# ScalarE makes the first part of p for the third block of rows

## The chip, the cores and the metric

The kernel runs on one core of a Trainium2 chip. The metric is the device time of one execution in microseconds (us). A core has a matrix engine (TensorE, PE in the profile; its weight loads are PEld), VectorE (DVE), ScalarE (ACT), GpSimd (POOL) and SyncE (SP), whose queue issues the DMAs here. Each engine takes its instructions in order; between engines they wait for semaphores.

## The reference

Three layers in a row. Attention with a decay for 4 batches of 8 heads, sequence 576, head width 64:

```python
scores = scale * np.matmul(q, k.transpose(0, 1, 3, 2))
decay = cum[:, :, :, None] - cum[:, :, None, :]      # cum: running sum of log f
scores = np.where(causal, -1000000000.0, scores + decay)
attn = np.exp(scores - max); attn = attn / (sum + 1e-09)
out = np.matmul(attn, v)
```

Then a first MLP (512 to 2048 and back, with a leaky ReLU that has a slope per column), and a second one (512 to twice 1536, the two halves multiplied, back to 512), over 2304 tokens.

## The kernel before

The work is float32 throughout; most products are made of two or three products of rounded parts. 32 heads pass through attention one after the other, numbered n, in steps u = 0 to 33. The 576 rows of a head are four blocks of 128 rows (i = 0 to 3) and a rest of 64, which two heads share (i = 4). Causality makes block i 128 x (i + 1) wide, so the third block (i = 2) is 128x384.

One step works on three heads: it makes the scores of head u and their exponentials (ops s0 to s3; VectorE takes the scores from PSUM, adds the mask and finds the maximum, L385; ScalarE takes the exponential and its sum, L386), normalises head u - 1 and turns it (ops h0 to h4 and l0 to l4), and multiplies head u - 2 by v (p0, p1). Op T turns q and k of head u + 1 (L338) and copies them out of PSUM in parts (L346 to L358). Op ri, first in each step, makes the reciprocals of the sums on VectorE (L408, L409); the h ops need them.

The normalised exponentials are called p. There are two kinds of heads:

- In the first ten heads (n below NATIVE, 10) p stays whole. Op h multiplies s by the reciprocal in place (L421 to L428), op l transposes it on TensorE (L449) and copies it out of PSUM.
- In the other 22 heads p is split into two half precision parts. Op h makes the first part, s times the reciprocal rounded to 16 bits (L436 to L440); op l makes the second, the remainder, on VectorE (L520). When both blocks of a group are done, a DMA transposes the group (L527). Blocks 2 and 3 are one group, p_hi, blocks 0 and 1 another, p_lo.

Which engine runs an op is read from a table by `eng`. Its default for the h ops is GpSimd:

```python
def eng(key, default):
    d = _P["eng"]
    if ap_["u"] < _P.get("es", 0):
        d = dict(d, **_P.get("eng0", {}))
    return {"pool": pool, "act": act, "dve": dve}[d.get(key, default)]
```

`es` is 10: in steps 0 to 9 the entries of `eng0` are laid over the table. `eng0` has no entry for h2.

The strings `even`, `odd`, `even0` and `odd0` list the ops of a step in the order in which the text issues them; h2 stands behind h3 in the odd steps and in the later even ones. Op M, once step 10 is reached, lets blocks of the first MLP in between, at a rate that the table fixes, so that TensorE has work while softmax runs; op W rounds weights. The MLP blocks use ScalarE for a ReLU and a rounding copy (L668, L670), VectorE for the leaky sum (L669) and GpSimd for the remainder (L671). The text's order gives priorities; the framework's scheduler, which keeps a timeline of its own costs (L1078), writes the order of each engine's queue from them, and adds the semaphores.

After attention the rest of the first MLP and then the second run, which the table does not touch.

Of the kernel before, what the change touches and what calls it, by code (L numbers as in the profile page):

```python
# [40 lines left out]
    odd="ri h3 h2 h0 R rr vs h1 M Q l2 T l3 s2 M h4 s3 l1 M M s1 l0 s0 p0 p1 V W po l4 M".split(),  # L41
    split=0,
    lag=2,
    eng={'U': 'pool', 'xl': 'pool', 'h0': 'pool', 'h1': 'pool', 'nq': 'act', 'x': 'dve'},
    psm=3,
    first=10,
    rates=[0, 1, 1, 1, 0.8, 1.15, 1.15, 0.95],
# [1034 lines left out]
```

## Time and profile before

| | us |
|---|---|
| median of 3 runs | 1085.79 (1085.08 to 1087.99) |
| profiled execution | 1083.83 |
| its span, first to last instruction | 1082.0 |
| TensorE busy | 1027.9 |
| VectorE busy | 719.0 |
| ScalarE busy | 473.8 |
| GpSimd busy | 516.8 |

Busy time is the union of an engine's instructions; the rest of the span is idle time, and the profile names for it what the next instruction waited for. The granted clock is the share of TensorE's full speed that it was given: it has two levels, 2.4 and 1.2 GHz, and its mean over the execution was 0.992.

### The profile page before, as it was taken

The page shows a single profiled execution, that of the slowest core. Times are in us where ns is not written, and L with a number is a line of the kernel's source. Part 1 is how long each engine was busy: PE and PEld are TensorE (multiplying, and loading weights), DVE is VectorE, ACT ScalarE, POOL GpSimd, SP SyncE. Part 2 cuts the span into 40 slices and gives each one's busy share as a digit, 9 for nine tenths or more (in the row PEclk, how much of TensorE's full clock was granted, in tenths as well). Part 3 has the DMA queues.
Part 4 walks back from the last instruction along what each step waited for, and adds up shares of the span by engine and source line. Part 5 has one row for each costly group of instructions (what it writes and reads, how often), then busy time and mean ns, then how long its engine had stood idle before and what let it go on. Part 6 is the DMA issues. An engine that isn't in the chain of part 4 may idle for free.

```text
span 1082.0 us, 18604 instructions
## 1 busy us (share of the span) xinstructions
PE 1027.9 (95%) x6447; PEld 963.6 (89%) x6447; DVE 719.0 (66%) x1518; ACT 473.8 (44%) x1168; POOL 516.8 (48%) x598
## 2 busy tenths in 40 slices
PE   5989999999999999999999997899999999999998
PEld 3868888898888899999999996899989999899997
DVE  6667988888888456444456358654986568974553
ACT  5777767767675454333344443322433113321110
POOL 4444767667676356333446667522443223541111
PEclk9999899999999999999999999999999999999999
DMA  5546575875775676666666997636327483354623
GB/s 113 154 101 193 123 132 123 201 146 116 176 163 100 165 262 192 192 223 199 191 215 227 355 365 257 238 134 253 108 88 254 155 301 126 124 183 172 241 86 111
DMA packets 221697, 196.26 MB, mean 181 GB/s; under 512 B 138980, under 2 KB 195812, under 8 KB 221604
## 3 DMA queue, kind: packets, MB, share of 16 engines
q1 hardware_dynamic: 221604, 195.08, 60.0%
q8 instruction: 51, 0.84, 0.3%
q14 instruction: 42, 0.34, 0.1%
HBM read 126.83 MB, written 50.17 MB: 164 GB/s over the span
## 4 chain that ended last, share of the span: by engine, by line
PE 55%; DVE 5%; POOL 2%; DMA 2%; issue 2%; ACT 1%; SPq 0%; ACTq 0%; DVEq 0%; POOLq 0%
PE p L674 7%; PE p L676 7%; PE p L675 7%; PE o L676 4%; PE o L675 4%; PE o L674 4%; PE hb L674 4%; PE ya L675 3%; PE hb L676 3%; PE hb L675 3%; PE ya L676 3%; PE ya L674 3%; DMA wr_in<-in_moe_w_in 1%; POOL yhl L881 1%; POOL g L671 0%
## 5 line engine op out<-in xcount | busy, mean ns | idle before, releaser
L674 PE MATMUL p<-yq,w_h 128*128 128x384 f32 x360 | 122.4, 340 | 4.7 <-DVE td L1031 2.3
L675 PE MATMUL p<-yq,w_h 128*128 128x384 f32 x360 | 121.8, 338 | 0.0
L676 PE MATMUL p<-yq,w_h 128*128 128x384 f32 x360 | 121.2, 338 | 0.0
L1015 POOL TENSOR_TENSOR gg<-tc,gg 128x384 fp32r<-128x384 f32 x36 | 36.6, 1017 | 113.2 <-ACT gg L1014 102.9
L674 PE MATMUL o<-w_o,gg 128*128 128x512 f32 x216 | 85.2, 396 | 3.4 <-ACT gg L1014 3.4
L675 PE MATMUL o<-w_o,gg 128*128 128x512 f32 x216 | 85.6, 396 | 0.0
L671 POOL TENSOR_TENSOR gb<-lt,gb 128x384 fp32r<-128x384 f32 x54 | 56.0, 1038 | 60.3 <-ACT gb L670 60.2
L676 PE MATMUL o<-w_o,gg 128*128 128x512 f32 x216 | 84.0, 394 | 0.5 <-POOL gg L1015 0.5
L386 ACT ACTIVATE s<-s,nm 128x512 f32<-128x512 f32 (+3 forms) x128 | 71.5, 559 | 26.3 <-DVE nm L385 25.2
L1015 POOL TENSOR_TENSOR gg<-td,gg 128x384 fp32r<-128x384 f32 x36 | 37.6, 1044 | 93.2 <-ACT gg L1014 87.4
L674 PEld LDWEIGHTS p<-yq,w_h 128*128 128x128 f32 x360 | 68.0, 189 | 9.4 <-issue 2.2
L669 DVE SCALAR_TENSOR_TENSOR lt<-lu,nal,hb 128x384 f32<-128x384 f32 x54 | 33.0, 612 | 61.5 <-ACT lu L668 61.5
L1014 ACT CAST gg<-tc 128x384 fp32r<-128x384 f32 x36 | 18.5, 514 | 123.8 <-DVE tc L1013 123.3
L675 PE MATMUL ya<-gb,w_out 128*128 128x384 f32 x216 | 72.7, 337 | 0.0
L676 PE MATMUL ya<-gb,w_out 128*128 128x384 f32 x216 | 72.3, 336 | 0.0
L674 PE MATMUL h<-xh,w_in 128*128 128x288 f32 x224 | 68.0, 307 | 3.5 <-DVE lt L669 3.5
L674 PE MATMUL ya<-gb,w_out 128*128 128x384 f32 x216 | 71.2, 335 | 0.0
L675 PEld LDWEIGHTS p<-yq,w_h 128*128 128x128 f32 x360 | 67.8, 188 | 3.5
L675 PE MATMUL y<-g,w_out 128*128 128x288 f32 x224 | 67.7, 306 | 2.0 <-POOL g L671 1.8
L674 PE MATMUL y<-g,w_out 128*128 128x288 f32 x224 | 66.8, 307 | 1.4 <-DVE lt L669 1.0
L676 PEld LDWEIGHTS p<-yq,w_h 128*128 128x128 f32 x360 | 67.5, 188 | 0.2
L675 PE MATMUL h<-xl,w_in 128*128 128x288 f32 x224 | 66.9, 300 | 0.1
(206 smaller groups left out, 3318.3 us busy)
## 6 DMA issues: line engine op xcount, KB each, us to landing
yq<-yq_d SPq DMA_DIRECT2D x49, 768.0 KB
yq_d<-yhl SPq DMA_DIRECT2D x42, 384.0 KB
yl<-ya_d SPq DMA_DIRECT2D x48, 192.0 KB
po_d<-os SPq DMA_DIRECT2D x36, 256.0 KB
os<-po_d SPq DMA_DIRECT2D x36, 256.0 KB
wr_in<-in_moe_w_in SPq DMA_DIRECT2D x16, 512.0 KB
wr_out<-in_moe_w_out SPq DMA_DIRECT2D x16, 512.0 KB
wr_a<-in_moe_w_a SPq DMA_DIRECT2D x12, 512.0 KB
```

The costliest lines, as they stand in the source:

```text
L386: act.activation(s, s, AF.Exp, bias=nm, scale=-1.0, accum_out=sm)
L669: dve.scalar_tensor_tensor(t, u, nal[:, fi:fi + 1], hp[:, :n], op0=ALU.mult, op1=ALU.add)
L671: pool.tensor_tensor(gl, t, f32(gh), op=ALU.subtract)
L674: pe.matmul(o, lh, rh, start=start, stop=False)
L675: pe.matmul(o, lh, rl, start=False, stop=False)
L676: pe.matmul(o, ll, rh, start=False, stop=stop)
L881: pool.tensor_tensor(yh[:, 1], x, f32(yh[:, 0]), op=ALU.subtract)
L1014: ap_["last"] = act.copy(g[:, 0], o).ins
L1015: pool.tensor_tensor(g[:, 1], o, f32(g[:, 0]), op=ALU.subtract)
```

## The change

One entry is added to the table, so that `eng("h2", "pool")` returns ScalarE:

```diff
-    eng={'U': 'pool', 'xl': 'pool', 'h0': 'pool', 'h1': 'pool', 'nq': 'act', 'x': 'dve'},
+    eng={'U': 'pool', 'xl': 'pool', 'h2': 'act', 'h0': 'pool', 'h1': 'pool', 'nq': 'act', 'x': 'dve'},
```

`p_hi` (L417) reads it in both of its branches. In either, GpSimd's product of s with the reciprocal becomes ScalarE's activation Copy with the reciprocal as its scale:

```python
if e is act:
    act.activation(t[:, 0::2, :], s, AF.Copy, scale=ri)
else:
    e.tensor_scalar(t[:, 0::2, :], s, ri, 1.0, op0=ALU.mult, op1=ALU.mult)
```

## Rows read from the trace of the kernel before

**Rows 1.** The page: busy time, share of the span and instructions.
```profile
PE 1027.9 (95%) x6447; PEld 963.6 (89%) x6447; DVE 719.0 (66%) x1518; ACT 473.8 (44%) x1168; POOL 516.8 (48%) x598
```

**Rows 2.** Windows: stretch, length, busy us of each engine, clock, DMA share, GB/s.
```profile
24.00:118.00 94.00, 87.28 (x553) 72.23 (x552) 65.47 (x206) 69.76 (x194) 46.61 (x65) 1.00 0.52 143
118.00:362.00 244.00, 226.14 (x1966) 213.04 (x1964) 210.54 (x559) 166.34 (x491) 166.34 (x238) 0.99 0.68 142
124.00:136.00 12.00, 10.79 (x56) 10.23 (x56) 11.32 (x35) 9.85 (x31) 7.34 (x10) 0.72 0.76 166
364.00:368.00 4.00, 4.00 (x21) 4.00 (x20) 0.00 (x0) 0.80 (x2) 0.00 (x0) 0.57 0.47 104
```

**Rows 3.** TensorE's waits: 118 to 362 us, then two of 24 to 118.
```profile
PE pv L542 <- DVE nm L385: 5.3, 9, 1.7
PE h L674 <- DVE lt L669: 2.9, 2, 1.5
PE sc L372 <- DVE nm L385: 2.6, 4, 1.0
PE pv L542 <- ACT TU L234: 2.0, 4, 0.7
...
PE sc L369 <- ACT PT_hi L234: 1.0, 2, 0.8
PE tp L449 <- POOL w_out L140: 0.8, 1, 0.8
```

**Rows 4.** Groups of GpSimd by form: busy us, mean ns, idle before.
```profile
L440 POOL TENSOR_SCALAR p_hi<-s,ri 128x384 f16<-128x384 f32 x22 | 12.9, 584 | 0.0
L427 POOL TENSOR_SCALAR s<-s,ri 128x384 f32<-128x384 f32 x10 | 6.2, 615 | 4.6 <-DVE ri L409 4.6
```

**Rows 5.** Timeline, end of attention: start us, us, instruction, idle before it.
```profile
359.03 0.58 POOL L440 TENSOR_SCALAR p_hi<-s,ri 128x384 f16<-128x384 f32 x1
362.84 0.78 POOL L671 TENSOR_TENSOR g<-lt,g 128x288 fp32r<-128x288 f32 x1
363.67 0.40 PE L675 MATMUL y<-g,w_out 128*128 128x288 f32 x1 [1.82 <-POOL g L671]
```

**Rows 6.** Line 427 on GpSimd: who waited for it (us, times).
```profile
  PEld tp L449: 2.2, 2
```

**Rows 7.** Groups of ScalarE by form, 118 to 362 us.
```profile
L386 ACT ACTIVATE s<-s,nm 128x384 f32<-128x384 f32 x21 | 12.9, 615 | 11.0 <-DVE nm L385 10.4 <-POOL p_lo L440 0.6
L234 ACT CAST xh<-x 128x320 fp32r<-128x320 f32 x10 | 4.6, 461 | 0.8 <-DVE x L576 0.5
```

**Rows 8.** Timeline of ScalarE and VectorE around the head at 288 us.
```profile
284.73 0.62 ACT L386 ACTIVATE s<-s,nm 128x384 f32<-128x384 f32 x1
285.25 0.19 ACT L386 ACTIVATION_READ_ACCUMULATOR s<-s,nm 128x1 f32 x1
287.61 0.38 ACT L575 ACTIVATE x<-pv 64x256 f32<-64x256 f32 x1
287.82 0.18 DVE L409 RECIPROCAL ri<-sm 128x4 f32<-128x4 f32 x1
288.49 0.41 ACT L234 CAST xh<-x 128x256 fp32r<-128x256 f32 x1 [0.51 <-DVE x L576]
```

**Rows 9.** Windows: the two microseconds behind ri in two heads.
```profile
152.50:154.50 2.00, 2.00 (x17) 2.00 (x16) 0.94 (x3) 1.90 (x7) 1.87 (x3) 1.00 1.17 203
322.50:324.50 2.00, 1.40 (x13) 1.19 (x11) 1.11 (x2) 1.90 (x5) 1.43 (x3) 1.00 0.73 176
```

**Rows 10.** Timeline of GpSimd and VectorE in two heads.
```profile
145.02 0.75 DVE L520 SCALAR_TENSOR_TENSOR p_hi<-s,ri,p_hi 128x512 f16<-128x512 f32 x1
...
288.83 0.59 POOL L440 TENSOR_SCALAR p_hi<-s,ri 128x384 f16<-128x384 f32 x1
288.89 1.06 DVE L520 SCALAR_TENSOR_TENSOR p_hi<-s,ri,p_hi 128x512 f16<-128x512 f32 x1 [0.43 <-POOL p_hi L440]
```

**Rows 11.** Groups of VectorE by form, 118 to 362 us.
```profile
L520 DVE SCALAR_TENSOR_TENSOR p_hi<-s,ri,p_hi 128x512 f16<-128x512 f32 x22 | 21.6, 981 | 5.4 <-POOL p_hi L440 5.3
```

**Rows 12.** Line 440 on GpSimd: duration ns min/median/max.
```profile
L440 POOL TENSOR_SCALAR p_lo<-s,ri x44: 365/772/1052, 119.8 to 360.4; 128x128 f16<-128x128 f32 x22, 128x256 f16<-128x256 f32 x22
```

## The prediction

> **What bounds the kernel now.** I read the page's busy line first, then the windows by stage, then who TensorE waits for. The busy line [rows 1] shows TensorE busy in 95% of a 1082.0 us span, VectorE in 66%, ScalarE in 44%, GpSimd in 48%; the average hides the stages. The change acts only while attention runs, up to about 362 us. There [rows 2] TensorE is busy 87.3 of 94 us between 24 and 118 us (the heads with whole p, no MLP blocks yet to fill in) and 226.1 of 244 us between 118 and 362 us (the heads with split p, interleaved with MLP blocks). So 6.7 and 17.9 us of TensorE idle are what can be won there at most, beside a slower clock; the matmuls themselves are fixed by the text. In the second stretch VectorE is busy 210.5 of 244 us, ScalarE and GpSimd 166.3 each. The waits of TensorE [rows 3] say which neighbour is late: the three largest entries are VectorE's (5.3 + 2.9 + 2.6 = 10.8 of the 17.9 us), the largest of ScalarE's is 2.0. In the first stretch ScalarE's entry is 1.0 and GpSimd's 0.8, both single or double stalls. VectorE is the neighbour that sets the pace of the split heads, ScalarE and GpSimd have some 78 us of slack each.
>
> **The change, part by part.** The key h2 is read at one place for both kinds of head, and the early table of engines does not overrule it. So all 32 heads move, the ten with whole p as well as the 22 with split p, though the words speak of the split ones alone. Nothing else is added: no DMA, no tile, no buffer.
>
> *What GpSimd loses.* 22 x 0.584 = 12.9 us in the split heads and 10 x 0.615 = 6.2 us before them [rows 4]. GpSimd is not the bound, so this counts only where something waits for it. One place is plain: at the end of attention GpSimd makes h2 of the last head at 359.03, four more instructions after it, and at 362.84 the subtraction that TensorE has been waiting for since 361.85; TensorE resumes at 363.67 after 1.82 us idle [rows 5]. Without h2 this comes 0.58 us sooner: -0.6 us (bounds 0, if ScalarE's part delays it instead, and -1.82). The other is at the start: TensorE's weight loads for the transposes waited twice, 2.2 us together, for GpSimd's rows of p [rows 6], and GpSimd makes the rows of one head one after the other. Two stalls shorter by up to 0.58 us each is -1.2 at best; I take -1.0 (bounds 0 and -1.2).
>
> *What ScalarE gains.* No row shows a scaled copy of 128x384 from SBUF to half precision. From above it is bounded by the exponential of the same 128x384, 0.615 us, which also takes a per-partition operand; from below by the 128x320 rounding copy, 0.461 us, with fewer columns and no such operand [rows 7]. The nearest is the exponential. Its neighbours overlap it: started at 284.73, its successor began at 285.25 [rows 8], so 0.52 us of the queue is what I charge: 22 x 0.52 = 11.4 us and 10 x 0.52 = 5.2 us. It waits for the reciprocal ri on VectorE. What is queued behind it on ScalarE: the copies of the next head's q and k out of PSUM, the high part of x, the ReLUs and rounding copies of the MLP, later the exponentials. VectorE and then TensorE wait for these. In the head at 288 us there is a hole for it: ScalarE ends its copy of x at 287.99 and idles 0.51 us until 288.49 while ri is ready at 288.00 [rows 8]. In the heads whose ri comes at 152.5 and at 322.5 there is none: ScalarE is busy 1.90 of the next 2.00 us [rows 9]. Going through all 22 in this way, 8 have no hole over 0.15 us within 2 us of ri, and these two are the first and last of them. So 8 x 0.52 = 4.2 us is pushed on; I let a quarter reach TensorE, taking that half of what stands behind it (the exponentials) is waiting for VectorE in any case, and that half of what is then late finds TensorE still with work: +1.05 us (bounds 0 and all 11.4). In the ten early heads ScalarE is busier, 69.8 of 94 us [rows 2], and a quarter of 5.2 is +1.3 (bounds 0 and 5.2).
>
> *What VectorE gains.* Behind h3 on GpSimd comes h2, and in the same moment VectorE starts the low part of the fourth block, which reads the same SBUF. At 288.83 GpSimd starts h2 (0.59 us) and at 288.89 VectorE starts l3, which takes 1.06 us; the l3 at 145.02, with no h2 beside it, takes 0.75 [rows 10]. The mean over 22 is 0.981 [rows 11]. So at most 22 x (0.981 - 0.75) = 5.1 us of VectorE's time goes. But GpSimd then does the next product, h0, at that moment, and l3 meets this one: I let half return, and half of the rest reach TensorE, since VectorE also idles (33.5 of 244 us, [rows 2]): -1.25 us (bounds 0 and -5.1).
>
> The Trainium skill (SBUF — State Buffer, "Who interferes with whom") says that a VectorE instruction with two SBUF inputs and a GpSimd instruction that reads SBUF exclude each other, the first to start keeping the shared port for its whole length, and that ScalarE has ports of its own. The 1.06 against 0.75 us agrees in direction, though the surplus, 0.31, is less than the 0.53 us that h2 still had to run. By this rule h0 (0.37 us at its shortest [rows 12]) would block l3 in h2's place, so an estimate from the rule keeps 0.59 - 0.37 = 0.22 us per head, 4.8 us on VectorE, and by the same halving -2.4 instead of -1.25: the sum would be -1.65.
>
> *The sum.* -0.6 - 1.0 + 1.05 + 1.3 - 1.25 = -0.5 us. The profiled execution took 1083.83 us (span 1082.0 and 1.8 around it), so it would be 1083.3; the median shown is 1085.79, 1.96 above the profiled one, so I predict 1085.3 for the median. The order that the framework's scheduler writes is worked out anew with the moved instruction, so these terms will not fall exactly where they do now; the ends below are wide for that.
>
> **The rivals.** *Faster: VectorE's relief goes through whole.* Nearly all of TensorE's stalls in the split heads are released by VectorE [rows 3]; if each head's stall shrinks by what VectorE saves, -5.1 stands for -1.25. The stall at 363.67 [rows 5] is followed by four microseconds at a mean granted clock of 0.57, so mostly at the lower of the two levels, 1.2 GHz [rows 2]: 4 x 0.43 = 1.7 us lost; a shorter stall may spare it. Sum: -5.1 - 0.6 - 1.7 - 1.0 + 1.05 + 1.3 = -6.05, 1079.7. For it: rows 3. Against: ScalarE's waits for VectorE are long, so the chain has slack in it.
>
> *Slower: ScalarE's queue becomes the late one.* ScalarE takes its instructions in order, and h2 can't start before ri. Where it is put ahead of the q and k copies, they stand behind its wait and its 0.52 us, the next head's scores start late, and TensorE has no scores to fill with. If half of it reaches TensorE in all heads, 32 x 0.52 / 2 = +8.3 stands for the +2.35: 8.3 - 0.6 - 1.0 - 1.25 = +5.45, 1091.2. It decides from the point where more than about half of the heads have no hole on ScalarE (8 of 22 now). One more stretch like 124 to 136 us, 12 us at a mean clock of 0.72 [rows 2] after TensorE had stalled, would add 12 x 0.28 = 3.4. For it: ScalarE's 74% in the early heads. Against: 14 heads with a hole, and ScalarE's slack of 78 us.
>
> *It does not do what it says:* if the ten early heads stay on GpSimd, +1.3 - 1.0 falls away: -0.8, 1085.0. The code speaks against it.
>
> **How the numbers follow.** 0.3% is 3.3 us, about what can be told from no change here; it separates 1082.5 and 1089.1. Chances: the forecast 0.37, the faster rival 0.35, the slower 0.23, the last 0.05 (it falls within 0.3%). So faster 0.35, the same 0.42, slower 0.23. The ends of the unknown terms reach from -9.8 (-1.82 - 1.7 - 1.2 - 5.1) to +16.6 (11.4 + 5.2), but all on one side at once is unlikely; 1078 to 1092 takes in both rivals' values with about 1 in 10 left on either side. The forecast's own range is 1082.5 to 1089.
>
> **What would show it.** Right: 32 activations of 128x384 on ScalarE of 0.55 to 0.62 us, none on GpSimd; GpSimd's busy time between 118 and 362 us down by some 13 us, ScalarE's up by as much; l3's mean between 0.75 and 0.95 us; the idle of TensorE in both stretches within 3 us of 6.7 and 17.9; the stall before the last subtraction 0.6 us shorter; nothing moved after 404 us but its start. Wrong: TensorE's waits for ScalarE (TU, T, N, PT) above 6 us in the split heads, as the slower rival wants; or TensorE's waits for VectorE under 7 us, as the faster one does; or a stretch at the lower clock that comes or goes, which moves the time by 2 to 3 us whatever these terms do.

## The result, and the profile after

The changed kernel takes 1072.12 us (median, 1068.47 to 1075.31) against 1086.89 for the kernel before, timed beside it: a ratio of 0.9874, 95% interval 0.9846 to 0.9902. That is 13.7 us faster by the ratio, where 0.5 was forecast, and below the range, which ended at 1078.

The busy line of the page, beside [rows 1]:

```profile
PE 1023.1 (96%) x6447; PEld 959.4 (90%) x6447; DVE 708.1 (66%) x1518; ACT 488.7 (46%) x1200; POOL 498.1 (47%) x566
```

GpSimd lost 32 instructions and ScalarE gained 32: both kinds of heads moved. VectorE's instructions are the same 1518, and yet its busy time fell by 10.9 us. Where the time went is seen with windows cut at the same work in both kernels: from 24 us to the exponential of the eleventh head's fourth block, and from there to the last product of p and v. First before, then after:

```profile
24.00:115.70 91.70, 84.98 (x537) 70.03 (x536) 63.17 (x197) 67.51 (x187) 45.18 (x63) 1.00 0.52 141
115.70:372.20 256.50, 236.97 (x2051) 223.56 (x2051) 214.32 (x571) 171.29 (x504) 169.55 (x242) 0.98 0.68 141
```

```profile
24.00:117.10 93.10, 84.83 (x533) 69.78 (x532) 62.79 (x197) 70.99 (x196) 39.65 (x54) 1.00 0.50 139
117.10:359.00 241.90, 231.17 (x2054) 219.18 (x2054) 204.62 (x571) 181.21 (x526) 155.46 (x220) 1.00 0.74 150
124.00:136.00 12.00, 11.56 (x93) 11.00 (x92) 11.15 (x34) 10.28 (x32) 5.81 (x8) 1.00 0.88 154
```

The heads with whole p take 1.4 us longer. The split heads take 14.6 us less (256.5 to 241.9), and all the work behind them is only earlier: the span from the last product of p and v to the end is 709.8 us in the one and 709.7 in the other. Of the 14.6 us, TensorE's idle time is 8.8 (19.5 to 10.7), and its busy time 5.8, for the same products: the granted clock is 1.00 where [rows 2] have 0.72 in 12 us (3.4 us lost) and 0.57 in 4 (1.7 us lost). How much of the clock's part is the change's is open: the profiled execution of the changed kernel had a mean clock of 0.997, its three others 0.990, 0.995 and 0.990. VectorE is busy 9.7 us less. The groups of its l ops by form, before and after (the first form before is in [rows 11]):

```profile
L520 DVE SCALAR_TENSOR_TENSOR p_hi<-s,ri,p_hi 128x384 f16<-128x384 f32 x22 | 18.0, 817 | 0.2
L520 DVE SCALAR_TENSOR_TENSOR p_lo<-s,ri,p_lo 128x256 f16<-128x256 f32 x22 | 14.4, 654 | 0.2
L520 DVE SCALAR_TENSOR_TENSOR p_lo<-s,ri,p_lo 128x128 f16<-128x128 f32 x22 | 13.6, 618 | 0.1
L520 DVE SCALAR_TENSOR_TENSOR p_r<-sr,rir,p_r 128x640 f16<-128x640 f32 x11 | 12.9, 1174 | 3.7 <-POOL p_r L440 3.6
```

```profile
L520 DVE SCALAR_TENSOR_TENSOR p_hi<-s,ri,p_hi 128x512 f16<-128x512 f32 x22 | 18.5, 842 | 2.1 <-POOL p_hi L440 2.1
L520 DVE SCALAR_TENSOR_TENSOR p_hi<-s,ri,p_hi 128x384 f16<-128x384 f32 x22 | 15.0, 683 | 3.2 <-ACT p_hi L438 2.9
L520 DVE SCALAR_TENSOR_TENSOR p_lo<-s,ri,p_lo 128x256 f16<-128x256 f32 x22 | 14.4, 653 | 0.1
L520 DVE SCALAR_TENSOR_TENSOR p_lo<-s,ri,p_lo 128x128 f16<-128x128 f32 x22 | 13.1, 595 | 1.2 <-POOL p_lo L440 1.0
L520 DVE SCALAR_TENSOR_TENSOR p_r<-sr,rir,p_r 128x640 f16<-128x640 f32 x11 | 10.8, 977 | 2.9 <-POOL p_r L440 2.9
```

Together these were 80.5 us (with the 21.6 of [rows 11]) and are 71.8: 8.7 us less for the same 99 instructions. Three of the five forms became shorter, not the fourth block's alone. TensorE's waits after, in the split heads, beside [rows 3]:

```profile
PE pv L542 <- DVE nm L385: 4.1, 5, 1.7
PE sc L372 <- DVE x L576: 2.5, 4, 1.3
PE h L675 <- POOL xl L582: 1.1, 1, 1.1
```

The stall of 1.82 us of [rows 5] is gone from the list; 0.3 us are left of it. The three kinds of waits for VectorE that the prediction added up, 10.8 us, are now 4.7: under the 7 us that it named as the faster rival's sign. All waits for VectorE together fell from 14.7 to 7.2. The mean of the fourth block's l op, 0.842, is where the forecast wanted it (0.75 to 0.95). What ScalarE now does, as groups, and in the timeline of one head:

```profile
L438 ACT ACTIVATE p_hi<-s,ri 128x384 f16<-128x384 f32 x22 | 13.6, 616 | 6.2 <-DMA PT_hi<-p_hi 2.8 <-POOL g L671 2.2 <-DVE ri L409 0.9
L425 ACT ACTIVATE s<-s,ri 128x384 f32<-128x384 f32 x10 | 6.1, 612 | 2.0 <-DVE ri L409 2.0
```

```profile
270.45 0.18 DVE L409 RECIPROCAL ri<-sm 128x4 f32<-128x4 f32 x1
270.80 0.62 ACT L438 ACTIVATE p_hi<-s,ri 128x384 f16<-128x384 f32 x1 [0.18 <-DVE ri L409]
271.32 0.42 ACT L575 ACTIVATE x<-pv 64x320 f32<-64x320 f32 x1
271.45 1.31 DVE L520 SCALAR_TENSOR_TENSOR p_hi<-s,ri,p_hi 128x384 f16<-128x384 f32 x2 [0.38 <-ACT p_hi L438]
271.46 1.64 POOL L440 TENSOR_SCALAR p_lo<-s,ri 128x128 f16<-128x128 f32 x2
```

h2 takes 0.62 us and holds the queue for 0.52 (270.80 to 271.32), as charged. In this head VectorE starts with the third block, whose first part now comes from ScalarE, and only then makes the fourth; the scheduler has turned them round. So it is in 15 of the 22 heads, and in none of the kernel before.

### The profile page after: what moved, and what is told of

The parts are those of the page before. It is cut to its first block, busy times and chain, and to the rows that moved or that the text cites. A ratio compares the mean times of both kernels' runs of the same rounds, so it can differ in the third digit from the quotient of the medians.

```text
span 1068.7 us, 18618 instructions
## 1 busy us (share of the span) xinstructions
PE 1023.1 (96%) x6447; PEld 959.4 (90%) x6447; DVE 708.1 (66%) x1518; ACT 488.7 (46%) x1200; POOL 498.1 (47%) x566
## 4 chain that ended last, share of the span: by engine, by line
PE 48%; DMA 6%; DVE 6%; POOL 3%; issue 3%; ACT 1%; SPq 0%; ACTq 0%; POOLq 0%; DVEq 0%
PE p L674 7%; PE p L676 7%; PE p L675 7%; PE o L676 4%; PE o L675 4%; PE o L674 4%; DMA yq_d<-yhl 4%; PE hb L674 2%; PE hb L676 2%; PE hb L675 2%; PE ya L675 2%; PE ya L676 2%; PE ya L674 2%; POOL yhl L881 2%; DMA wr_in<-in_moe_w_in 1%
## 5 line engine op out<-in xcount | busy, mean ns | idle before, releaser
L675 PE MATMUL y<-g,w_out 128*128 128x288 f32 x224 | 66.9, 301 | 0.5 <-POOL g L671 0.3
L385 DVE CUSTOM_DVE_ANT_0 s<-sc,maskz 128x512 f32<-128x512 f32 (+3 forms) x128 | 59.3, 485 | 10.8 <-PE sc L369 9.8
```

The costliest lines, as they stand in the source:

```text
L385: dve.tensor_tensor_reduce(s, o, m, -0.125, 3.0e38, ALU.add, ALU.min, nm)
L675: pe.matmul(o, lh, rl, start=False, stop=False)
```

## The experiments

**Theory.** GpSimd's reading of SBUF holds up VectorE's l ops, and VectorE sets the pace of the split heads, so its relief reaches TensorE whole. The runs bear out the first half; the second half is taken up under "Orders". **Rivals.** GpSimd's busy time, not its reads; the order that the scheduler writes anew with any edit; the gain in the early heads; ScalarE's cost.

**Which heads.** ScalarE in the split heads alone, or in the whole heads alone. (Behind each time stand the ratio to the kernel before, timed beside it, and its 95% interval.)

```diff
 # e1, in the branch for whole p; e2 has the same line in the branch for split p
-    e = eng(f"h{i}", "pool")
+    e = pool if i == 2 else eng(f"h{i}", "pool")
```

> ScalarE makes h2 in the 22 heads with split p alone; the ten with whole p keep it on GpSimd. The changed kernel reached the scores of the eleventh head 1.4 us later than before and ended attention 13.2 us sooner, so by the theory (VectorE's relief in the split heads goes through) the whole gain is here and a little more: 1.4 us better than the changed kernel's 1072, about 1071. If the gain is an accident of the order that the scheduler writes, it may come out anywhere between 1071 and 1087.

> ScalarE makes h2 in the ten heads with whole p alone. By the theory there is no gain in these: VectorE has no op there that reads SBUF beside GpSimd's h2, and ScalarE is the busier engine: 1085 to 1088, not faster. If the gain of the whole change were a new order after the tenth head, it could come out several us lower.

Measured: split alone 1072.82 (0.9889, 0.9875 to 0.9904), whole alone 1081.54 (0.9984, 0.9967 to 1.0). The gain is in the split heads: 12 us by the ratio in the first, 1.7 (0 to 3.6) in the second. The 1.4 us expected from leaving out the early heads did not show.

**Same order, read or write.** To keep the order out of it, two kernels were made whose queues on TensorE, VectorE, ScalarE and SyncE are instruction for instruction the same. Both are the changed kernel, with a scratch operation of GpSimd behind h3 in the split heads (cut; x stands for the scratch tile):

```diff
+    if i == 2:
+        with tc.issue_after(ap_["h", 3]):
+            pool.tensor_scalar(x[:, :384], x[:, 384:768], 1.0, 0.0, op0=ALU.mult, op1=ALU.add)  # e11
+            pool.memset(x[:, :540], 0.0)                                                        # e12 instead
```

> The changed kernel, and behind h3 in the split heads GpSimd copies 384 columns from one part of a scratch tile to another (nobody reads it). The queues of the four other engines are instruction for instruction those of the next kernel, so nothing but GpSimd's read of SBUF differs. If VectorE's l ops are held up by GpSimd's reads, the l op of the fourth block takes 0.95 to 1.0 us here and the time is 4 us or more above the next kernel's. If the order made the earlier difference of 5 us between reading and writing, the two agree within 1.5 us.

> The same as the kernel ahead of it, but GpSimd fills 540 columns of the scratch tile with zeros in place of the copy, which the scheduler takes to be as long: the same order on TensorE, VectorE, ScalarE and SyncE. By the theory about 1072 to 1073 and 0.80 to 0.85 us for the l op of the fourth block; by the rival (order) as the kernel ahead of it.

Measured: reading 1077.23 (0.9936, 0.9915 to 0.9956), writing 1073.12 (0.9892, 0.987 to 0.9914). Reading costs 4.1 us; the executions of the two do not overlap (1075.9 to 1078.9 and 1071.1 to 1073.5). The groups of the scratch operation and of the two l ops of p_hi, of the reading kernel and then of the writing one, and behind them the windows of the split heads in the same sequence:

```profile
L445 POOL TENSOR_SCALAR xtra<-xtra 128x384 f32<-128x384 f32 x22 | 13.8, 629 | 0.0
L525 DVE SCALAR_TENSOR_TENSOR p_hi<-s,ri,p_hi 128x512 f16<-128x512 f32 x22 | 19.6, 889 | 0.3 <-POOL p_hi L442 0.3
L525 DVE SCALAR_TENSOR_TENSOR p_hi<-s,ri,p_hi 128x384 f16<-128x384 f32 x22 | 18.3, 831 | 7.7 <-ACT p_hi L440 7.3
```

```profile
L445 POOL MEMSET xtra<- 128x540 f32 x22 | 12.1, 548 | 0.0
L525 DVE SCALAR_TENSOR_TENSOR p_hi<-s,ri,p_hi 128x512 f16<-128x512 f32 x22 | 18.8, 857 | 0.9 <-POOL p_hi L442 0.9
L525 DVE SCALAR_TENSOR_TENSOR p_hi<-s,ri,p_hi 128x384 f16<-128x384 f32 x22 | 15.6, 708 | 7.7 <-ACT p_hi L440 7.4
```

```profile
117.70:365.70 248.00, 233.49 (x2054) 219.52 (x2054) 209.56 (x571) 181.55 (x527) 169.52 (x242) 1.00 0.71 146
```

```profile
116.00:361.20 245.20, 233.06 (x2055) 219.50 (x2054) 206.07 (x573) 181.42 (x526) 164.97 (x242) 1.00 0.73 148
```

VectorE is busy 3.5 us longer with the read, TensorE idles 2.4 us longer (14.5 against 12.1) in the profiled executions, and VectorE's own idle time is nearly the same (38.4 and 39.1). The stretch is 2.8 us longer with the read; the two profiled executions lie 5.4 apart, and 1.7 of that was there at the start of the stretch, ahead of any scratch operation. So of one pair of executions only a part is the read's. It was the l op of the third block that grew (0.71 to 0.83), not the fourth block's, as the expectation had it: in this order it is the one that meets the copy most often, in 16 of 22 heads. The copy itself is held up too: its mean is 0.63 us, its median 0.51.

**The same two without that care about order**, run earlier; here the read is a second h2 into scratch, and the write 128x576 zeros (cut):

```diff
+    if i == 2:
+        pool.tensor_scalar(scratch, s, ri, 1.0, op0=ALU.mult, op1=ALU.mult)      # e3
+        with tc.issue_after(ap_["h", 3]): pool.memset(scratch, 0.0)              # e4 instead
```

> The changed kernel, and GpSimd makes h2 as well in the split heads, into a scratch tile that nobody reads: ScalarE does the work, GpSimd is loaded as before. By the theory (GpSimd's reading of SBUF holds up VectorE's l ops) VectorE's l ops go back to 0.95 us for the fourth block and the time to some 1082 to 1087. If only the load moved to ScalarE or the freed dependence counts, it stays at 1072.

> The changed kernel, and GpSimd fills a scratch tile of 128x576 with zeros behind h3 in the split heads (0.57 us, as long as h2 was): GpSimd is as busy as before but reads no SBUF in it. If VectorE is held up by GpSimd's reads, its l ops stay as short as in the changed kernel (0.84 us for the fourth block) and the time at 1072 to 1075. If it is GpSimd's busy time that counts (its queue later by 0.57 us a head), the time is that of the kernel before, 1083 to 1087.

Measured: 1077.81 (0.9945, 0.9927 to 0.9963) and 1072.89 (0.9889, 0.9873 to 0.9906). With the write GpSimd is busy 166.0 of 243.9 us in the split heads, in the changed kernel 155.5 of 241.9, and the time is the same: GpSimd's busy time does not count here. With the read the time came back by 5 (6 by the ratios), not by the whole 12, so the expected 1082 to 1087 was missed, though the fourth block's l op is as long as it was in the kernel before. It is shown with the read and then with the write:

```profile
L523 DVE SCALAR_TENSOR_TENSOR p_hi<-s,ri,p_hi 128x512 f16<-128x512 f32 x22 | 21.9, 998 | 2.2 <-POOL p_hi L441 2.0
```

```profile
L524 DVE SCALAR_TENSOR_TENSOR p_hi<-s,ri,p_hi 128x512 f16<-128x512 f32 x22 | 17.8, 811 | 0.3 <-POOL p_hi L441 0.3
```

**Orders.** h3 and h2 exchanged, in the kernel before and in the changed one:

```diff
-    even="ri T h3 h2 h0 ...   odd="ri h3 h2 h0 ...
+    even="ri T h2 h3 h0 ...   odd="ri h2 h3 h0 ...
```

> The kernel before with the ops h3 and h2 exchanged in the order of a step, both on GpSimd: no engine's load changes, only the order. It measures what a newly written order does by itself. By the theory 1087 within 3 us. If the gain of the change is an accident of the order, this may move the time by as much, 5 us or more either way.

> The changed kernel with the ops h3 and h2 exchanged in the order of a step. Exchanged in the kernel before, it gave 7 us. By the theory the two engines now work side by side, so the exchange changes little but the written order: 1072 within 4 us. If the change's gain and the exchange's were two gains that add, 1065.

Measured: 1077.93 (0.9938, 0.9923 to 0.9953), and 1070.35 (0.9873, 0.9847 to 0.9898). So a new order alone moved the kernel before by 7 us, and the changed one by hardly any; for the first 1087 within 3 had been expected, a miss. VectorE's l ops did not become cheaper by it; the groups of the exchanged kernel before show that the delay went from the fourth block to the third:

```profile
L520 DVE SCALAR_TENSOR_TENSOR p_hi<-s,ri,p_hi 128x384 f16<-128x384 f32 x22 | 21.3, 969 | 5.0 <-POOL p_hi L440 4.8
L520 DVE SCALAR_TENSOR_TENSOR p_hi<-s,ri,p_hi 128x512 f16<-128x512 f32 x22 | 18.7, 848 | 0.2
```

All 99 l ops together take 81.0 us here and 80.5 in the kernel before. From 24 us to the last product of p and v, the kernel before and then the exchanged one:

```profile
24.00:372.20 348.20, 321.95 (x2586) 293.60 (x2585) 277.49 (x767) 238.80 (x690) 214.73 (x304) 0.99 0.63 141
```

```profile
24.00:364.40 340.40, 319.92 (x2587) 290.42 (x2586) 276.48 (x769) 237.89 (x690) 217.14 (x304) 0.99 0.65 145
```

TensorE idles 5.8 us less (26.3 to 20.5) while VectorE is busy only 1.0 us less. So TensorE's idle time can fall without a relief of VectorE, and the near match of 8.8 and 9.7 us in the result does not show by itself that VectorE's relief goes through whole.

**ScalarE's cost**, in the kernel before:

```diff
+    if i == 2:
+        act.activation(scratch, s, AF.Copy, scale=ri)
```

> The kernel before, and ScalarE makes h2 as well in the split heads, into a scratch tile that nobody reads: the cost to ScalarE without the relief. I charged 0.52 us a head and let 1.05 us reach TensorE; so 0 to 2 us slower than before. By the rival with ScalarE's queue as the late one, 4 us or more slower.

Measured: 1084.32 against 1083.63 (1.0005, 0.9988 to 1.0021): nothing that can be told (0.5 us slower, between 1.3 faster and 2.3 slower). The rival with ScalarE's queue falls.

**Which of the split heads.** With heads 30 and 31, 10 and 11, or 12 to 29 on ScalarE, the rest on GpSimd, in the branch for split p:

```diff
-    e = eng(f"h{i}", "pool")
+    e = act if i == 2 and n >= 30 else eng(f"h{i}", "pool")     # e15: 10 <= n < 12; e16: 12 <= n < 30
```

> ScalarE makes h2 in the last two heads alone (30 and 31); the other thirty are as before. With two other kernels it divides the 22 split heads into three parts. The stall of 1.82 us before 363.67 shrinks by GpSimd's 0.58 us, and the 3.4 us at half speed behind it may go too: 0.6 to 2.3 us faster than before. If the gain is spread evenly over the 22 heads, 13 x 2 / 22 = 1.2.

> ScalarE makes h2 in the first two split heads alone (10 and 11). If the 6.8 us at half speed from 136.6 us go, 3.4 us faster; spread evenly, 1.2 us; if both hang on later heads, nothing.

> ScalarE makes h2 in the split heads 12 to 29 alone. By the theory (VectorE's relief goes through to TensorE head by head) 18 of 22 parts of the 8.7 us that VectorE's l ops lost, so 6 to 8 us faster than before, while the stretches at half speed at the two ends stay. If the clock and the ends made most of the gain, under 3 us.

(The 136.6 us of the second are on another axis; in the rows it is the stretch inside 124 to 136.) Measured against 1083.63: the last two 1082.28 (0.9986, 0.9972 to 1.0001), the first two 1079.92 (0.9966, 0.9952 to 0.9981), the middle 1074.16 (0.9916, 0.9884 to 0.9948). The last stall before the end, in the first of these:

```profile
362.21 0.40 PE L675 MATMUL y<-g,w_out 128*128 128x288 f32 x1 [1.25 <-POOL g L671]
```

1.25 us in place of 1.82: the 0.57 that h2 took, as worked out. The first two heads gave 3.7 us, as much as the stretch at half speed costs; but the mean clock of the stretch in their profile is 0.86 where it was 0.72, so only half of its cost is gone, and the rest of the gain came from elsewhere:

```profile
124.00:136.00 12.00, 10.56 (x68) 9.74 (x68) 11.85 (x36) 10.22 (x32) 7.54 (x10) 0.86 0.75 166
```

In the same profile the last stall is as long as in the kernel before, and the clock behind it is full:

```profile
360.81 0.40 PE L675 MATMUL y<-g,w_out 128*128 128x288 f32 x1 [1.83 <-POOL g L671]
```

```profile
364.00:368.00 4.00, 4.00 (x49) 3.79 (x48) 0.43 (x1) 1.18 (x3) 0.20 (x1) 1.00 0.24 78
```

The middle 18 heads gave the most, 9.1 us by the ratio (5.6 to 12.6), where 6 to 8 was expected. The three add to 14 against the 12 of all 22 at once; the intervals are too wide to tell the two apart.

**What is left beside the read.** The load of the reading kernel (e3), but with the l op of the third block taking GpSimd's copy of h2 as before; and second orders of e3 and e5 (h3 and h2 exchanged, as above):

```diff
+    first = scratch if i == 2 else t[:, 0::2, :]
-    ...scalar_tensor_tensor(t[:, 1::2, :], s, ri, t[:, 0::2, :], ...)
+    ...scalar_tensor_tensor(t[:, 1::2, :], s, ri, first, ...)
```

> As the kernel in which GpSimd makes h2 as well (1077.8), but the l op of the third block on VectorE takes GpSimd's copy of h2, not ScalarE's: the load of every engine is the same, only what the l op waits for is as in the kernel before. If its waiting behind h3 and h2 on GpSimd is what is left of the gain, 1081 to 1085. If the rest of the gain lies in the written order or the clock, 1076 to 1079.

> The kernel in which ScalarE makes h2 and GpSimd makes it as well for nobody (1077.8), with h3 and h2 exchanged in the order: a second written order of the same work. If orders scatter the time by several us, it lies well away from 1077.8; with reading as the cause of the loss, it stays 4 us or more above the exchanged changed kernel's 1070.4.

> The kernel before with ScalarE making h2 for nobody (1084.3), with h3 and h2 exchanged: a second written order of that work. The exchange alone gave 7 us in the kernel before; if this gain belongs to h2 being first on GpSimd it comes again, 1077 to 1079; if it was an accident of one order, 1082 to 1087.

Measured: 1079.65 (0.9958, 0.9942 to 0.9974), 1079.78 (0.9961, 0.9943 to 0.9978) and 1082.79 (0.999, 0.9981 to 1.0). The first lies between the two ranges that were expected: the wait of the l op is worth some 2 us at most, no more than a second order of the same work (1077.8 and 1079.8). The second is 9.4 us above the exchanged changed kernel (1070.35), which differs from it by GpSimd's scratch h2 alone; 4 or more was expected of the read. The exchange's 7 us did not come again (1084.3 to 1082.8): most of them belonged to one order.

**One more read moved**, h0 on ScalarE too:

```diff
-    'h2': 'act', 'h0': 'pool',
+    'h2': 'act', 'h0': 'act',
```

> The changed kernel with h0 on ScalarE too (128x128 in each split head; in the first ten heads h0 stays on GpSimd only where the early table says nothing, so it moves there as well). If GpSimd's reads hold up VectorE, moving one more of them gives 1 to 3 us: 1069 to 1071. If ScalarE is at its limit now, slower than 1072.

Measured: 1079.07 (0.996, 0.9946 to 0.9975), 7 us slower than the change alone (9 by the ratios): a miss. Its l ops, as groups, and then the wait of TensorE that is new:

```profile
L520 DVE SCALAR_TENSOR_TENSOR p_hi<-s,ri,p_hi 128x512 f16<-128x512 f32 x22 | 21.5, 978 | 1.3 <-POOL p_hi L440 1.2
L520 DVE SCALAR_TENSOR_TENSOR p_hi<-s,ri,p_hi 128x384 f16<-128x384 f32 x22 | 16.7, 761 | 2.8 <-ACT p_hi L438 2.6
```

```profile
PE y L674 <- ACT g L670: 2.9, 4, 1.1
```

With less on GpSimd the fourth block's l op is as long as in the kernel before: other reads of GpSimd stand beside it in this order. And TensorE waits 2.9 us for ScalarE's rounding copies, where the change alone has 0.4. Which of the two weighs more was not tried.

**All together.** Fourteen kernels differ only in who makes h2, in scratch work and in order. In the five whose GpSimd reads nothing behind h3 for h2 (the change, e1, e4, e7, e12) the medians are 1070.4 to 1073.1. In the nine whose GpSimd reads 384 columns there (the kernel before, e2, e3, e5, e6, e11, e17, e18, e19) they are 1077.2 to 1086.9. The two do not overlap, over orders that differ in each. The kernels with some heads of each kind (e14 to e16) are not counted; and e9, which has neither h2 nor h0 on GpSimd, is at 1079.07, in the range of the nine. So the number of GpSimd's reads does not fix the time by itself.

## Why the prediction was wrong

**The step that failed** is the term "What VectorE gains": -1.25 us, with a bound of -5.1. It was mis-sized in three ways. It counted the l op of the fourth block alone, because that is the one that stands beside h2 in the rows; all the l ops together gave back 8.7 us. It let half return through h0; the order turned instead, and in 15 of 22 heads VectorE began with the third block, whose first part ScalarE had made. And it let half of the rest reach TensorE, because VectorE idled 33.5 us; at equal order, 2.4 of VectorE's 3.5 us came out as idle time of TensorE (e11 against e12), and the read cost 4.1 us, more than three times the term. Why the l ops of the third block and of the rest that two heads share became shorter too is argued, not shown: an l op that is late can meet GpSimd's next read.

**The order** is a term that the sum put at nothing. The prediction said that the scheduler would write the order anew and made its range wide for it; exchanging h3 and h2 moved the kernel before by 7 us (e6), as much as half of the whole change.

**The clock.** The sum had none of the 5.1 us that the two stretches cost; the faster rival had 1.7 of them, and the signs of being wrong said that such a stretch may come or go. Both are gone in the profile after, 5.1 of its 14.6 us. But the changed kernel's profiled execution had the highest mean clock of its four (0.997, 0.990, 0.995, 0.990), and the kernel before has a median of 0.993 in its later executions, so these 5.1 us are not shown to be part of the 13.7. Nor do the stretches simply come and go with TensorE's stalls: in the kernel before they follow 1.7 us of stalls between 122 and 126 us and the one of 1.82, but in e15 the clock behind a stall of 1.83 is 1.00, and the changed kernel has a stall of 1.68 us at 143.7 without one. The whole heads' kernel (e2), whose split heads are as before, has a clock of 1.00 from 124 to 136. What brings them stays open.

**The rival "faster"** had VectorE's relief going through whole, with 1079.7 at a chance of 0.35. It was nearer than the forecast, and its sign (waits for VectorE under 7 us, by the three kinds counted) came; but it too took the fourth block's l op alone and put the order at nothing, and its time lies 7.6 us above the measured one.

**What held.** ScalarE's 0.52 us a head, and that little of it reaches TensorE (e5). The early heads: +0.3 forecast, 1.4 us later in the profile, nothing that can be told in e1. The stall at the end: 0.6 us where the last two heads alone moved (e14); in the change 1.5 of the 1.82 are gone. GpSimd's saved time as such: nothing (e4, e12). Nothing moved behind attention but its start.

**The read and the write.** Reading behind h3 costs 4.1 us against writing, at the same order, and the kernel that writes is about as fast as the change itself. This is what the Trainium skill (SBUF — State Buffer, "Who interferes with whom") says of an instruction of VectorE with two SBUF inputs: it contends with a GpSimd instruction that reads SBUF, not with one that only writes it. The prediction's estimate from that rule, -2.4, was nearer than my -1.25, and still short of 4.1.

**What stays open.** Of the 12 us in the split heads, 4.1 are shown to be the read, at one order; two looser pairs, whose orders may differ, give 5 (e3 against e4) and 9 (e18 against e7). With the read put back, 4 to 7 us of the gain are left (e18, e3, e11), and no run says how much of this is the order, the clock or the moved wait (some 2 us at most by e17). Kernels with the same reads scatter over 7 us and more, those without over 3. That a schedule with fewer collisions scatters less is what the fourteen suggest; it was not tried by itself.

## What to carry to other kernels

When two engines share something, what one of them loses is read from all its instructions of that kind against their shortest (here 23.5 us over the 99 l ops before, 14.7 after), not from the one that stands beside the moved instruction. How much of that reaches the engine behind it is not read from idle time: VectorE idled 33.5 us, and still two thirds of what it lost came out at TensorE in the one pair with the order held fixed. Look at the clock of several executions before a gain at the higher clock is credited to the change. And where a scheduler writes the order, run a second order of the same work, or a pair at the same order, before a gain of some 1% is put down to the edit.

## What the runs showed of the hardware

VectorE's l ops and GpSimd's reads of SBUF lengthen each other, of the same rows or of others. The 128x384 l op took 0.60 us at its shortest (in the kernel before); with GpSimd's copy behind h3 its mean was 0.83, with GpSimd's zeros of the same length in its place 0.71. The copy itself took 0.51 us (median) and 0.63 (mean). In the kernel before, the five l ops of 128x256 that no instruction of GpSimd overlaps took 0.47 us, the other 17 took 0.71 on the mean. A scaled Copy of 128x384 on ScalarE, SBUF to half precision, takes 0.616 us and holds its queue for 0.52. The mean granted clock of one and the same kernel, the changed one, lay between 0.990 and 0.997 in four executions. Exchanging two neighbouring instructions in the text, with the same load on every engine, moved the time by 7 us once and by 1.5 to 2 us in the three other kernels.
